# Keeping all five W_q blocks of the first group in SBUF, with a smaller weight store, in a two-layer decode kernel

## Chip, cores and metric

The kernel runs on one core of one Trainium2 chip. The metric is device time in microseconds (us): the median of the runs of the whole program, lower is better. The program before takes 736.22 us (median of 3 runs, 736.16 to 736.47).

## What is computed

Four rows of 640 floats pass twice through the same two sublayers, all in float32 and with the same weights in both layers: a layer norm, attention over the last 1024 positions of a key and value cache (32 heads of 128), and a projection; then a layer norm and a gated MLP with 1728 hidden units. Each sublayer adds to its input.

```python
def _A_ref(x, k_cache, v_cache, wq, wo):        # B=4, D=640, Hq=32, Dh=128, W=1024
    q = (x @ wq) ...                            # per head
    scores = einsum("bhqd,bhkd->bhqk", q, k[last W]) * Dh ** -0.5
    o = einsum("bhqk,bhkd->bhqd", softmax(scores), v[last W])
    return o @ wo
def _B_ref(x, W_gate, W_up, W_down):
    gate = x @ W_gate; gate = gate * (gate > 0)
    return (gate * (x @ W_up)) @ W_down
x = x + _A_ref(_layernorm(x), ...); x = x + _B_ref(_layernorm(x), ...)   # twice
```

## The kernel before

**Data.** Host code lays all weights and caches out as three rows of 128 partitions: `heads` (groups 0 to 6 of heads, 255,744 floats a partition), `kept` (the last two groups, 47,360 floats) and `mlp` (25,920 floats). "Floats" below always counts floats per partition; one float on 128 partitions is 512 bytes. The nine groups hold 4, 4, 4, 4, 4, 4, 3, 3 and 2 heads (`HEADS`, L27). Line 38 sets the order inside `heads`: W_q and keys of the first group, then for each group g the W_q of g+2, the keys of g+1, the output weights of g-1 and the values of g. A head has 4096 floats of keys, 4096 of values and 640 of output weights; W_q of a group of four has 2560, in five blocks of 512.

**Store.** SBUF holds one large tile, `store` (53,888 floats, L103), and `first_q` (1024 floats, L104), which keeps the first two of the five W_q blocks of group 0 from the start to the end, so that layer 1 reads them again without a load. Everything else passes through `store`. `load()` (L157) walks a fixed list of pieces (L130 to L147) and issues one DMA for each on SP's queue, in that order and on no other queue. `heads` and `mlp` pieces go to the running position `at`, which starts at `FIRST` and goes back to 0 at the end of the store; a large piece is cut at the marks in `QUARTERS`. `kept` pieces always go to their own place, 0 to 47,360 (`FRONT`), and stay for layer 1, where groups 7 and 8 come first. The first `kept` piece is W_q of groups 7 and 8, 3200 floats to places 3200 to 6400, and it stands in the list just before the keys of group 6 (L131; `turn[0]` is the start of these keys). During the first MLP, whose pieces go through the ring between `FRONT` and the end of the store, the `kept` part is resident.

**What a load waits for.** The Python list `live` notes which places hold data that no instruction has read yet. `done()` frees places after a block's matmul has been emitted, and calls `load()` again, which issues the next piece only if the whole target is free (only at a few places, with `part=True`, may it take a shorter piece). So a piece is issued behind the last reader of what lies in its place, and all later pieces stand behind it. Here "block" is 512 floats with the one matmul that reads them, which TensorE runs as two passes, so that a count in the profile is twice the number of blocks.

**Order on TensorE.** For each group g of a layer (L422): transposes of the softmax rows, W_q of g+2 (`query`, L317 and L322), keys of g+1 (`scores`, L346), output weights of g-1 (`project`, L404), values of g (`values`, L374). The MLP (L446) goes through the blocks of its four column groups (L458), then of W_down (L493, L502). Small per-row numbers (sums, maxima, reciprocals) live in tiles of one or 16 floats.

Of the kernel before, what the change touches and what calls it, by code (L numbers as in the profile page):

```python
# [7 lines left out]
F32 = mybir.dt.float32  # L8
# [4 lines left out]
B, D, H, DH, W, F = 4, 640, 32, 128, 1024, 1728  # L13
P = 128
KC = D // P
# [12 lines left out]
SIDE = 4  # L28
# [28 lines left out]

HELD = 1024  # L60
STORE = 53888
QUARTERS = [STORE // 4, STORE // 2, STORE // 4 * 3, STORE]
FRONT = KEPT * 2 * (D + KV)
FIRST, FIRST_MLP = 10944, 53248


def size_of(what, i):
# [23 lines left out]
def decode_kernel(ctx: ExitStack, tc: tile.TileContext, x, source, sel, out):  # L91
    nc = tc.nc
    const = ctx.enter_context(tc.tile_pool(name="const", bufs=1))
    work = ctx.enter_context(tc.tile_pool(name="work", bufs=1))
    small = ctx.enter_context(tc.tile_pool(name="small", bufs=2))
    ps_s = ctx.enter_context(tc.tile_pool(name="ps_s", bufs=1, space=bass.MemoryType.PSUM))
    ps_p = ctx.enter_context(tc.tile_pool(name="ps_p", bufs=2, space=bass.MemoryType.PSUM))
    ps_o = ctx.enter_context(tc.tile_pool(name="ps_o", bufs=1, space=bass.MemoryType.PSUM))
    ps_y = ctx.enter_context(tc.tile_pool(name="ps_y", bufs=1, space=bass.MemoryType.PSUM))
    ps_m = ctx.enter_context(tc.tile_pool(name="ps_m", bufs=2, space=bass.MemoryType.PSUM))  # L100
    big = ctx.enter_context(tc.tile_pool(name="big", bufs=1))
    big.tile([P, 8], F32, name="pad")
# [34 lines left out]
    pieces(0, "kept", 0, 2 * D, 4 * D, KEPT * D)  # L137
    pieces(0, "mlp", 0, 1152, *range(GU0, WD0 + 1, 1280), WD1, *range(WD1 + 2 * D, MLP - D, 2 * D), MLP - D, MLP)
    k = at_part("k", 0)
    pieces(1, "heads", HELD, 2560, 3584, k, *range(k + 1536, k + 4 * 1536 + 1, 1536))  # L140
    wanted = [3072, 6144, 9216, 13312, 17408, 22016, 27136, 32256, 38912]
    pieces(1, "heads", k + 4 * 1536, *[max(c for c in ROWS["heads"][2] if c <= k + 4 * 1536 + w) for w in wanted],
           k + 50176)
# [13 lines left out]
    def load(part=False):  # L157

        nonlocal at, spare
        if not held:  # L160
            nc.sync.dma_start(out=first_q, in_=source["heads"][:, :HELD])
        while todo:
# [66 lines left out]
    xT = const.tile([P, KC * B + 28], F32, name="xT")  # L229


    qT = const.tile([P, SIDE - 1 + SIDE * SIDE * B], F32, name="qT")
    GAP = SIDE * B - B
    pT = [const.tile([P, GAP + 8 * SIDE * B], F32, name=f"pT{i}") for i in range(2)]
    for t in xT, qT, *pT:
# [6 lines left out]
    eps_sb = const.tile([P, 1], F32, name="eps_sb")  # L242
    nc.vector.memset(eps_sb, EPS)

    ident, sel_q = sel_sb[:, :P], sel_sb[:, P:]
# [25 lines left out]
    def normalized():  # L271

        ysb, xc, sq = probs[:, :QUARTER], gates[:, :QUARTER], gates[:, QUARTER:2 * QUARTER]
        waits[0] = True
        su = small.tile([P, 1], F32, name="su", bufs=1)
# [5 lines left out]
        ss = small.tile([P, 1], F32, name="ss", bufs=1)  # L281
# [8 lines left out]
        nc.vector.tensor_copy(xT[:, :KC * B].rearrange("p (c b) -> p c b", b=B), pt[:, :, :B])  # L290
        return ss

    def deviation(ss):
        var = mean(ss, "var")
        rs = small.tile([P, 1], F32, name="rstd")
        nc.scalar.activation(rs, var, AF.Sqrt, bias=eps_sb)
        nc.vector.reciprocal(rs, rs)
        return rs

    def table(func):  # L300

        t = small.tile([P, 1], F32, name="t", bufs=1)
        nc.scalar.activation(t, eps_sb, func)

    def go_on():

# [2 lines left out]
    qp, nm, sums, pps, r, oT = {}, {}, {}, {}, {}, {}  # L309
# [29 lines left out]
    def scores(layer, g):  # L339
        n = len(HEADS[g])  # L340
        for i, h in enumerate(HEADS[g]):
            for j in range(2):
                for b in range(B):
                    lo = (j * B + b) * 512
                    at = SIDE - 1 + SIDE * (B * i + b) - i
                    nc.tensor.matmul(ps[32 * b:32 * b + SIDE, j, :], qT[:, at:at + SIDE], part(layer, "k", h, lo, 512),  # L346
                                     start=i == 0, stop=i == n - 1, tile_position=(0, 32 * b))
                    part_done(layer, "k", h, lo, 512)
        nm[g] = small.tile([P, 1], F32, name="nm")
        nc.vector.tensor_reduce(nm[g], ps.rearrange("p j n -> p (j n)"), axis=AX.X, op=ALU.max, negate=True)  # L350

    def softmax(g):
        sums[g] = small.tile([P, 1], F32, name="sm")
# [54 lines left out]
    def attention(layer):  # L408
        gs = order[layer]
        load(True)  # L410
        rstd = deviation(normalized())
        table(AF.Exp)
        query(layer, gs[0], True)
        query_out(gs[0], rstd)
        query(layer, gs[1])
        query_turned(gs[0])
        go_on()
        query_out(gs[1], rstd)
        scores(layer, gs[0])
        softmax(gs[0])  # L420
        query_turned(gs[1])
        for before, g, after, then in zip([None] + gs, gs, gs[1:] + [None], gs[2:] + [None] * 2):  # L422
            totals(g)
            turned(g)
            if before is not None:
                values_turned(before)
            if then is not None:
                query(layer, then)
                query_out(then, rstd)
            if after is not None:  # L430
                scores(layer, after)
                softmax(after)
            else:
                table(AF.Sqrt)
            if then is not None:
                query_turned(then)

            if before is not None and not (layer == 0 and after is None):
                project(layer, before)
            values(layer, g, after is None)  # L440
        values_turned(gs[-1])
        if layer == 0:
            project(layer, gs[-2])
        project(layer, gs[-1], True)

    def forward(layer):  # L446
        load(True)
        ss = normalized()
        gus, hTs = {}, {}

        def gate(j):
# [21 lines left out]
            return b  # L473

        def hidden(j, h):
            hTs[j] = small.tile([P, 4, B], F32, name="hT", bufs=4)
            ph = ps_m.tile([P, 4, 32], F32, tag="m", name="ph")
            if j < 3:
                nc.tensor.transpose(ph, h, ident)
                nc.vector.tensor_copy(hTs[j], ph[:, :, :B])  # L480
                return

            for g, lo, f in (0, 0, 0), (1, 64, 0), (2, 0, 1), (2, 64, 1):
                nc.tensor.matmul(ph[lo:lo + 64, f, :B], h, ident[:96, 32 * g:32 * g + B],
                                 start=True, stop=True, tile_position=(0, lo))
            nc.vector.tensor_copy(hTs[j][:, :2], ph[:, :2, :B])
# [18 lines left out]

        gate(3)
        waits[0] = layer == 0
        rstd = deviation(ss)
        go_on()
        h = gated(3)  # L510
        for j, j1 in (3, 0), (0, 1), (1, 2):
# [72 lines left out]
```

## Time and profile before

| what | number |
|---|---|
| median of 3 runs | 736.22 us |
| the profiled execution, its own time | 736.33 us |
| its span (first to last instruction) | 734.5 us |
| TensorE matmul, busy | 452.5 us (62%) |
| VectorE, ScalarE busy | 75.0 us, 47.1 us |
| mean granted TensorE clock | 0.83 |
| read from HBM | 312.24 MB, 425 GB/s over the span |

The profile is of one execution on the chip. Busy time is given by engine; PEld is TensorE's weight load, SPq is SP's queue, from which the DMAs are issued. The line "DMA" gives the share of time in which the 16 DMA engines were busy. A row of the timeline has the start, the length, the engine, the line, what is written and read, the count, and in brackets the engine's idle time before and what ended it. A row of DMA issues has the target and source, the count, the size of one and the time from issue to landing.

### The profile page before, as it was taken

The numbers are of one execution on the slowest core, as the hardware profiler recorded it, in microseconds if no ns is written. First come the engines' busy times: TensorE is split into PE (matmuls) and PEld (weight loads), VectorE is DVE, ScalarE is ACT, GpSimd is POOL, SyncE is SP. The second block draws the span as 40 slices with busy tenths as digits, with TensorE's granted clock in tenths as the row PEclk, the third lists the DMA queues.
The fourth block names the chain that finished last, engine by engine and source line by source line (L and its number), as shares of the span: only waits on it lengthen the run. The fifth ranks groups of instructions, "written<-read, shape, count | busy, mean of one in ns | idle before, by whom it ended". The sixth has DMA issues, their size and how long they took to land.

```text
span 734.5 us, 8243 instructions
## 1 busy us (share of the span) xinstructions
PE 452.5 (62%) x3749; PEld 142.7 (19%) x3749; DVE 75.0 (10%) x279; ACT 47.1 (6%) x88; POOL 0.2 (0%) x4
## 2 busy tenths in 40 slices
PE   1657366555566635727789897446756545656686
PEld 0111111111121201202233231101211111122242
DVE  1011010010000101101101221001010100001010
ACT  1100000000000000000101110000000000000110
POOL 0000000000000000000000000000000000000000
PEclk9989787867678887969899999867878977668897
DMA  9999999999999999999999999999999999999996
GB/s 380 454 421 430 452 430 422 429 446 434 417 444 445 408 446 419 438 433 419 419 405 406 432 433 431 445 432 443 431 427 425 447 432 424 435 445 429 420 427 285
DMA packets 15738, 312.85 MB, mean 426 GB/s; under 512 B 1748, under 2 KB 2132, under 8 KB 7512
## 3 DMA queue, kind: packets, MB, share of 16 engines
q1 hardware_dynamic: 15552, 312.24, 99.1%
q8 instruction: 29, 0.48, 0.2%
q10 hardware_dynamic: 152, 0.09, 0.1%
q14 instruction: 5, 0.04, 0.0%
HBM read 312.24 MB, written 0.08 MB: 425 GB/s over the span
## 4 chain that ended last, share of the span: by engine, by line
DMA 54%; PE 30%; another core or an unknown queue 14%; issue 1%; DVE 1%; ACT 0%; SPq 0%; DVEq 0%; ACTq 0%
DMA store<-in_heads 32%; PE ps L346 12%; DMA store<-in_mlp 12%; DMA store<-in_kept 10%; PE po L374 9%; PE y L404 1%; PE qp L317 1%; PE pp L359 1%; PE qp L322 1%; PE gu L458 1%; PE qt L334 1%; PE ot L394 0%; PE po L259 0%; PE y L493 0%
## 5 line engine op out<-in xcount | busy, mean ns | idle before, releaser
L346 PE MATMUL ps<-store,qT 128*4 128x512 f32 x1024 | 160.9, 700 | 108.2 <-DMA store<-in_heads 104.3
L374 PE MATMUL po<-store,pT 128*16 128x512 f32 x1024 | 155.2, 718 | 105.4 <-DMA store<-in_heads 95.4
L374 PEld LDWEIGHTS po<-store,pT 128*16 128x16 f32 x1024 | 35.0, 110 | 210.8 <-issue 128.3
L346 PEld LDWEIGHTS ps<-store,qT 128*4 128x4 f32 x1024 | 29.4, 94 | 221.6 <-DMA store<-in_heads 119.9
L350 DVE TENSOR_REDUCE nm<-ps 128x1 f32<-128x1024 f32 x18 | 22.0, 1224 | 245.0 <-PE ps L346 245.0
L354 ACT ACTIVATE probs<-ps,nm 128x1024 f32<-128x1024 f32 x18 | 20.1, 1114 | 353.6 <-DVE nm L350 345.9
L317 PE MATMUL qp<-store,xT 128*32 128x512 f32 (+2 forms) x136 | 22.9, 614 | 24.7 <-DMA store<-in_heads 24.6
L404 PE MATMUL y<-store,oT 128*4 128x160 f32 x512 | 26.2, 335 | 8.7 <-DMA store<-in_heads 7.6
L458 PE MATMUL gu<-store,xT 128*32 128x256 f32 (+1 forms) x300 | 26.3, 414 | 8.3 <-DMA store<-in_mlp 7.9
L370 DVE COPY pT<-pp 128x16 f32<-128x16 f32 x128 | 17.1, 168 | 135.3 <-PE po L374 135.3
L381 ACT COPY gates<-po 128x512 f32<-128x512 f32 x16 | 9.4, 587 | 243.1 <-PE po L374 243.1
L359 PE MATMUL pp<-sel_sb,probs 128*128 128x128 f32 x144 | 19.5, 281 | 0.0
L322 PE MATMUL qp<-store,xT 128*32 128x512 f32 (+4 forms) x48 | 17.7, 514 | 0.0
L327 DVE TENSOR_SCALAR gates<-qp,rstd 128x512 f32<-128x512 f32 (+2 forms) x18 | 12.4, 691 | 48.4 <-PE qp L322 44.4
L359 PEld LDWEIGHTS pp<-sel_sb,probs 128*128 128x128 f32 x144 | 17.1, 146 | 0.0
L404 PEld LDWEIGHTS y<-store,oT 128*4 128x4 f32 x512 | 13.3, 93 | 19.5 <-DMA store<-in_heads 8.0
L387 DVE RECIPROCAL r<-so 128x16 f32<-128x16 f32 x18 | 4.6, 257 | 121.4 <-PE so L385 121.4
L458 PEld LDWEIGHTS gu<-store,xT 128*32 128x32 f32 x300 | 11.4, 123 | 18.9 <-issue 8.7
L394 PE MATMUL ot<-sel_sb,gates 128*128 128x128 f32 x72 | 11.7, 283 | 1.2 <-DVE gates L378 1.2
L334 PE MATMUL qt<-sel_sb,gates 128*128 128x128 f32 x64 | 12.3, 316 | 0.0
L493 PE MATMUL y<-store,hT 128*4 128x160 f32 x208 | 10.6, 305 | 1.7 <-DMA store<-in_mlp 1.7
L334 PEld LDWEIGHTS qt<-sel_sb,gates 128*128 128x128 f32 x64 | 7.6, 155 | 18.8 <-issue 17.5
(62 smaller groups left out, 107.2 us busy)
## 6 DMA issues: line engine op xcount, KB each, us to landing
store<-in_heads SPq DMA_DIRECT2D x18, 6656.0 KB, 54.0
store<-in_heads SPq DMA_DIRECT2D x7, 6912.0 KB, 52.0
store<-in_heads SPq DMA_DIRECT2D x2, 6592.0 KB, 54.4
store<-in_heads SPq DMA_DIRECT2D x2, 5376.0 KB, 65.4
store<-in_mlp SPq DMA_DIRECT2D x16, 640.0 KB, 6.9
store<-in_kept SPq DMA_DIRECT2D x4, 2048.0 KB, 39.9
store<-in_heads SPq DMA_DIRECT2D x3, 2560.0 KB, 22.0
store<-in_heads SPq DMA_DIRECT2D x1, 6896.0 KB, 46.1
```

The lines of the kernel that those rows point to most:

```text
L317: nc.tensor.matmul(qp[g][32 * c:32 * c + 32, :], xT[:, B * c:B * c + 32], part(layer, "q", g, c * n, n), start=True, stop=c > 0 and not sp ...
L322: nc.tensor.matmul(qp[g][32 * a:32 * a + 32, a * m:a * m + m], xT[:, B * c:B * c + 32], part(layer, "q", g, c * n + a * m, m), start=False ...
L327: nc.vector.tensor_scalar(gates[:, :len(HEADS[g]) * P], qp.pop(g), rstd, SCALE, op0=ALU.mult, op1=ALU.mult)
L334: nc.tensor.transpose(qt[:, i], gates[:, i * P:(i + 1) * P], ident)
L346: nc.tensor.matmul(ps[32 * b:32 * b + SIDE, j, :], qT[:, at:at + SIDE], part(layer, "k", h, lo, 512), start=i == 0, stop=i == n - 1, tile_ ...
L350: nc.vector.tensor_reduce(nm[g], ps.rearrange("p j n -> p (j n)"), axis=AX.X, op=ALU.max, negate=True)
L354: nc.scalar.activation(probs, ps.rearrange("p j n -> p (j n)"), AF.Exp, bias=nm.pop(g), accum_out=sums[g])
L359: nc.tensor.transpose(pps[g][c // 4][:, c % 4, :], probs[:, c * P:(c + 1) * P], ident)
L370: nc.vector.tensor_copy(to[:, 4 * j:4 * j + 4], pp[j][:, :, i:P:32])
L374: nc.tensor.matmul(po[32 * a:32 * a + SIDE * B, :], t[:, at:at + SIDE * B], part(layer, "v", h, c * 512, 512), start=i == 0 and c < 4, sto ...
L404: nc.tensor.matmul(y[32 * a:32 * a + B], o[:, i], part(layer, "o", h, a * QUARTER, QUARTER), start=False, stop=last and h == HEADS[g][-1], ...
L458: nc.tensor.matmul(gus[j][32 * g:32 * g + 32, :2 * n], xT[:, B * c:B * c + 32], get(layer, "mlp", lo, 2 * n), start=c == 0, stop=c == KC - ...
```

## The change

`first_q` grows from 1024 to 2560 floats (all five blocks), and the store shrinks from 53,888 to 52,480. The marks in `QUARTERS` move, `FIRST` goes from 10,944 to 10,752 and the start of the first MLP to the last 640 floats of the smaller store, so that the ring of the first MLP between 47,360 and the end of the store has 5120 floats where it had 6528. Layer 1 loads `heads` from float 2560 on, not from 1024. To make room, the one-float tiles become columns of the tile `qT`, and `r`, `oT` and `hT` share four buffers.

```diff
-HELD = 1024
-STORE = 53888
-QUARTERS = [STORE // 4, STORE // 2, STORE // 4 * 3, STORE]
+HELD = KC * 4 * P
+STORE = 55040 - HELD
+QUARTERS = [13312, 2 * 13312, 3 * 13312, STORE]
-FIRST, FIRST_MLP = 10944, 53248
+FIRST, FIRST_MLP = 10752, STORE - 640
...
-    small = ctx.enter_context(tc.tile_pool(name="small", bufs=2))
+    small = ctx.enter_context(tc.tile_pool(name="small", bufs=4))
...
-    pieces(1, "heads", HELD, 2560, 3584, k, *range(k + 1536, k + 4 * 1536 + 1, 1536))
+    pieces(1, "heads", HELD, 3584, k, *range(k + 1536, k + 4 * 1536 + 1, 1536))
...
-    qT = const.tile([P, SIDE - 1 + SIDE * SIDE * B], F32, name="qT")
+    n = SIDE - 1 + SIDE * SIDE * B
+    qT = const.tile([P, n + 10], F32, name="qT")
+    ones = qT[:, n:]
+    qT = qT[:, :n]
...
+    eps_sb, su, ss, t1 = (ones[:, i:i + 1] for i in range(4))
+    rstds, nms, sms = ([ones[:, i + j:i + j + 1] for j in range(2)] for i in (4, 6, 8))
...
-        nm[g] = small.tile([P, 1], F32, name="nm")
+        nm[g] = nms[g % 2]
...
-        r[g] = small.tile([P, SIDE, B], F32, name="r")
+        r[g] = small.tile([P, 4, B], F32, tag="s", name="r")
...
-        oT[g] = small.tile([P, SIDE, B], F32, name="oT")
+        oT[g] = small.tile([P, 4, B], F32, tag="s", name="oT")
...
-            hTs[j] = small.tile([P, 4, B], F32, name="hT", bufs=4)
+            hTs[j] = small.tile([P, 4, B], F32, tag="s", name="hT")
```

The new sizes move where each piece lands in the store. The rows below give an instruction's line, kind, target and source, shape, and the semaphores it waits for: `DMAHW0` to `DMAHW7` tell that a DMA has landed (they are used in turn), `PE` that TensorE has passed a point. First SP's queue where the first `kept` piece stands, before:

```order
L186 DMA store<-in_heads 128x13824 [waits DMAHW7_49,DMAHW6_49,PE_49]
L186 DMA store<-in_heads 128x13312 [waits PE_49]
L186 DMA store<-in_heads 128x3072 [waits DMAHW0_49,PE_49]
L186 DMA store<-in_kept 128x3200 [waits PE_49]
L186 DMA store<-in_heads 128x6656 [waits PE_49]
L186 DMA store<-in_heads 128x13824 [waits DMAHW2_49,DMAHW1_49,PE_49]
L186 DMA store<-in_heads 128x10752 [waits PE_49]
```

And the same place of the changed kernel:

```order
L186 DMA store<-in_heads 128x13312 [waits DMAHW6_49,PE_49]
L186 DMA store<-in_heads 128x12288 [waits DMAHW7_49,PE_49]
L186 DMA store<-in_heads 128x7168 [waits DMAHW0_49,PE_49]
L186 DMA store<-in_kept 128x3200 [waits DMAHW4_49,PE_49]
L186 DMA store<-in_heads 128x6656 [waits PE_49]
L186 DMA store<-in_heads 128x13312 [waits DMAHW1_49]
L186 DMA store<-in_heads 128x11264 [waits DMAHW2_49]
```

The `heads` piece ahead of the `kept` one goes to the start of the store and has 7168 floats now, 3072 before; the `kept` row has gained a wait for a landing, `DMAHW4`.

On TensorE, the reader of that last `heads` piece is `values` of group 4 (L374). Before, its second half:

```order
L374 MATMUL po<-store,pT_99 16x512 x3
L374 MATMUL po<-store,pT_100 16x512 [waits DVE_49]
L374 MATMUL po<-store,pT_100 16x512
L374 MATMUL po<-store,pT_100 16x512 [waits DMAHW4_49]
L374 MATMUL po<-store,pT_100 16x512
L374 MATMUL po<-store,pT_100 16x512 [waits DVE_49]
L374 MATMUL po<-store,pT_100 16x512 x3
```

and in the changed kernel, with the group's third and fourth head whole:

```order
L374 MATMUL po<-store,pT_99 16x512 [waits DVE_49]
L374 MATMUL po<-store,pT_99 16x512
L374 MATMUL po<-store,pT_99 16x512 [waits DMAHW4_49]
L374 MATMUL po<-store,pT_99 16x512
L374 MATMUL po<-store,pT_99 16x512 [waits DVE_49]
L374 MATMUL po<-store,pT_99 16x512 x3
L374 MATMUL po<-store,pT_100 16x512 [waits DVE_49]
L374 MATMUL po<-store,pT_100 16x512 x3
L374 MATMUL po<-store,pT_100 16x512 [waits DVE_49]
L374 MATMUL po<-store,pT_100 16x512 x3
```

The wait for `DMAHW4` stands ahead of the last 14 blocks of the group now, ahead of the last six before.

Last, SP's queue at the start of the first MLP, as one piece of the difference:

```order
 L186 DMA store<-in_mlp 128x1280 [waits DMAHW3_49]
 L186 DMA store<-in_mlp 128x1280 [waits DMAHW4_49]
-L186 DMA store<-in_mlp 128x1280 [waits DMAHW5_49]
-L186 DMA store<-in_mlp 128x768 [waits DMAHW6_49]
-L186 DMA store<-in_mlp 128x512 [waits DMAHW7_49,DMAHW0_49,PE_49]
-L186 DMA store<-in_mlp 128x768 [waits DMAHW2_49,DMAHW1_49,PE_49]
+L186 DMA store<-in_mlp 128x512 [waits DMAHW5_49]
+L186 DMA store<-in_mlp 128x768 [waits DMAHW6_49,DMAHW0_49,PE_49]
+L186 DMA store<-in_mlp 128x768 [waits DMAHW2_49,DMAHW7_49,DMAHW1_49,PE_49]
 L186 DMA store<-in_mlp 128x512 [waits PE_49]
```

The first piece that waits for TensorE (`PE`) stands behind 4992 floats of this MLP now and behind 6528 before.

More of the change, by code (lines that the diff above doesn't have):

```diff
@@ L101, in decode_kernel @@
     big = ctx.enter_context(tc.tile_pool(name="big", bufs=1))
-    big.tile([P, 8], F32, name="pad")
+    big.tile([P, 16], F32, name="pad")
     store = big.tile([P, STORE], F32, name="store")
@@ L241, in decode_kernel @@
     nc.vector.memset(po, 0.0)
-    eps_sb = const.tile([P, 1], F32, name="eps_sb")
+    eps_sb, su, ss, t1 = (ones[:, i:i + 1] for i in range(4))
+    rstds, nms, sms = ([ones[:, i + j:i + j + 1] for j in range(2)] for i in (4, 6, 8))
     nc.vector.memset(eps_sb, EPS)
@@ L274, in normalized @@
         waits[0] = True
-        su = small.tile([P, 1], F32, name="su", bufs=1)
         nc.vector.tensor_reduce(su, y, axis=AX.X, op=ALU.add)
@@ L280, in normalized @@
         nc.vector.tensor_tensor(xc, ysb, mu.to_broadcast([P, QUARTER]), op=ALU.subtract)
-        ss = small.tile([P, 1], F32, name="ss", bufs=1)
         nc.scalar.activation(sq, xc, AF.Square, accum_out=ss)
@@ L290, in normalized, with deviation @@
         nc.vector.tensor_copy(xT[:, :KC * B].rearrange("p (c b) -> p c b", b=B), pt[:, :, :B])
-        return ss
-    def deviation(ss):
+    def deviation():
         var = mean(ss, "var")
-        rs = small.tile([P, 1], F32, name="rstd")
+        rs = rstds[0]
+        rstds.reverse()
         nc.scalar.activation(rs, var, AF.Sqrt, bias=eps_sb)
@@ L300, in table @@
     def table(func):
-        t = small.tile([P, 1], F32, name="t", bufs=1)
-        nc.scalar.activation(t, eps_sb, func)
+        nc.scalar.activation(t1, eps_sb, func)
     def go_on():
@@ L348, in scores @@
                     part_done(layer, "k", h, lo, 512)
-        nm[g] = small.tile([P, 1], F32, name="nm")
+        nm[g] = nms[g % 2]
         nc.vector.tensor_reduce(nm[g], ps.rearrange("p j n -> p (j n)"), axis=AX.X, op=ALU.max, negate=True)
     def softmax(g):
-        sums[g] = small.tile([P, 1], F32, name="sm")
+        sums[g] = sms[g % 2]
         nc.scalar.activation(probs, ps.rearrange("p j n -> p (j n)"), AF.Exp, bias=nm.pop(g), accum_out=sums[g])
@@ L410, in attention @@
         load(True)
-        rstd = deviation(normalized())
+        normalized()
+        rstd = deviation()
         table(AF.Exp)
@@ L447, in forward @@
         load(True)
-        ss = normalized()
+        normalized()
         gus, hTs = {}, {}
@@ L507, in forward @@
         waits[0] = layer == 0
-        rstd = deviation(ss)
+        rstd = deviation()
         go_on()
```

## The prediction, as it was made

> **What bounds the kernel now.** I read the page's first two parts first, to see which resource never rests.
>
> ```profile
> PE 452.5 (62%) x3749; PEld 142.7 (19%) x3749; DVE 75.0 (10%) x279; ACT 47.1 (6%) x88; POOL 0.2 (0%) x4
> DMA  9999999999999999999999999999999999999996
> ```
>
> TensorE is busy 62% of the span and VectorE 10%, but the DMA engines are full in every slice except the last. The windows say how full, from 20 us to the end of the loads, and in the stretch of layer 0 that the sum below needs:
>
> ```profile
> 20.00:725.00 705.00, 442.40 (x3596) 138.46 (x3588) 70.94 (x263) 42.57 (x82) 0.00 (x0) 0.82 1.00 430
> 100.00:340.00 240.00, 139.60 (x1070) 40.42 (x1074) 21.33 (x82) 10.75 (x18) 0.00 (x0) 0.78 1.00 431
> ```
>
> The last two columns are the DMA share and GB/s: 1.00 and 430 over 705 us. So the kernel is one unbroken stream of loads, and what follows the last of them is short. The chain of waits shows that end:
>
> ```profile
> 708.31 22.62 DMA store<-in_mlp
> 730.98 0.50 PE y L493 x8
> 731.50 0.32 DVE probs L524
> ```
>
> The last load lands at 730.9; matmuls and a copy of under 1 us follow, then the store of the output. Two things can therefore move the time: the number of bytes, and any moment in which the queue has nothing to transfer. A wait of TensorE by itself costs nothing.
>
> **What is removed.** Layer 1 no longer loads floats 1024 to 2560 of `heads`: 1536 floats x 512 bytes = 0.786 MB. At 430 GB/s that is **1.8 us** off the stream. Layer 0 loads the same bytes as before. At the start only the cut changes (2560 floats for `first_q`, not 1024), and TensorE is far from needing them:
>
> ```profile
> first_q<-in_heads SPq DMA_DIRECT2D x1, 512.0 KB, 3.9
> 18.17 1.07 PE L317 MATMUL qp<-first_q,xT 128*32 128x512 f32 x2 [0.20 <-DVE xT L290]
> ```
>
> The 1536 further floats land 1.8 us after 0.7 + 3.9 = 4.6 us, and the first reader starts at 18.2.
>
> **What is added: an empty queue ahead of the first `kept` piece.** The order rows of SP give the places. In the changed kernel `heads` fills the store from 10,752 to 52,224 in the first lap, to 52,224 in the second and third, and to 52,096 in the fourth; of the 207,744 floats ahead of the keys of group 6, 7168 are left, and they go to places 0 to 7168. They are the last 14 blocks of the values of group 4. The next piece in the list is `kept`, with places 3200 to 6400. These are inside the 7168. So this load can't be issued before the piece just ahead of it has landed and all but one of its 14 blocks have been read; hence the new `DMAHW4` in its row. SP's queue is in order, and all later loads stand behind it: the keys of group 6, two pieces of 13,312 and 11,264 floats, and so on. When the 7168 floats have landed, nothing is in flight. Before, the piece had 3072 floats, below 3200, and the target held only floats read long ago. The issue times show what is lost:
>
> ```profile
> 204.01 0.33 SPq L186 DMA_DIRECT2D store<-in_heads  x1
> 205.71 0.33 SPq L186 DMA_DIRECT2D store<-in_kept  x1
> ```
>
> ```profile
> store<-in_heads SPq DMA_DIRECT2D x1, 1536.0 KB, 46.3
> ```
>
> ```profile
> store<-in_kept SPq DMA_DIRECT2D x1, 1600.0 KB, 48.4
> ```
>
> The `heads` piece of 3072 floats (1536 KB) is issued at 204.0 and lands 46.3 us later, at 250.3; the `kept` piece is issued at 205.7, with 44.6 us of transfers ahead of it, and lands at 254.1. In the changed kernel the bytes up to this point are the same, so the 7168 floats land at 250.3 too, and only then does the reading begin.
>
> How fast TensorE reads them depends on its clock, so I look at this very place before:
>
> ```profile
> 231.06 6.94 PE L346 MATMUL ps<-store,qT 128*4 128x512 f32 x44 [6.84 <-DMA store<-in_heads]
> 237.93 0.55 PE L334 MATMUL qt<-sel_sb,gates 128*128 128x128 f32 x3
> 238.41 1.27 PE L404 MATMUL y<-store,oT 128*4 128x160 f32 x32
> 246.83 9.32 PE L374 MATMUL po<-store,pT 128*16 128x512 f32 x64 [7.15 <-DMA store<-in_heads]
> 257.64 0.85 PE L317 MATMUL qp<-store,xT 128*32 128x384 f32 x8
> ```
>
> ```profile
> 246.80:251.80 5.00, 4.97 (x28) 1.26 (x32) 0.35 (x2) 0.00 (x0) 0.00 (x0) 0.54 1.02 433
> 251.80:256.10 4.30, 4.30 (x45) 0.97 (x33) 0.35 (x2) 0.00 (x0) 0.00 (x0) 1.00 1.05 452
> ```
>
> After 7 us of idling TensorE gets half the clock for 5 us (0.54), then the full one. The weight loads show the pace in both states:
>
> ```profile
> 250.20 0.19 PEld L374 LDWEIGHTS po<-store,pT 128*16 128x16 f32 x4 [0.66 <-issue]
> 251.05 0.19 PEld L374 LDWEIGHTS po<-store,pT 128*16 128x16 f32 x4 [0.66 <-DVE pT L370]
> 252.53 0.12 PEld L374 LDWEIGHTS po<-store,pT 128*16 128x16 f32 x4 [0.31 <-issue]
> 252.96 0.12 PEld L374 LDWEIGHTS po<-store,pT 128*16 128x16 f32 x4 [0.31 <-DVE pT L370]
> ```
>
> Four passes are two blocks: 0.85 us at half clock, 0.43 at full, so 0.43 and 0.215 us a block. In the changed kernel the piece of 12,288 floats ahead lands 7168 x 512 bytes / 431 GB/s = 8.5 us earlier, at 241.8, and TensorE restarts there, at half clock until about 246.8. It has the last block of keys, the transposes and the projection to do (some 2 us at full clock by the rows above, 4 at half), then 18 blocks of values, two of them by 246.8 and 16 at 0.215: it is through at about 250.2, as the last piece lands, and goes on at full clock. The 13th block of it starts 12 x 0.215 = 2.6 us later and takes
>
> ```profile
> L374 PE MATMUL po<-store,pT x64: 592/592/1061, 246.8 to 255.6; 128*16 128x512 f32 x64
> ```
>
> 0.6 us at full clock and 1.06 at half (ns, least, median and most), so SP is released at 250.3 + 3.2 = **253.5**.
>
> What a load pays on an empty queue is not shown in mid-kernel. The nearest rows are the first load and the last store:
>
> ```profile
> 0.73 0.38 SPq L161 DMA_DIRECT2D first_q<-in_heads  x1
> 1.20:1.70 0.50, 0.00 (x0) 0.00 (x0) 0.29 (x2) 0.00 (x0) 0.00 (x0) 1.00 0.13 10
> 1.70:2.20 0.50, 0.00 (x0) 0.00 (x0) 0.50 (x1) 0.00 (x0) 0.00 (x0) 1.00 1.19 141
> ```
>
> ```profile
> out_x<-probs SPq DMA_DIRECT2D x1, 80.0 KB, 1.6
> ```
>
> `first_q` (0.52 MB) takes 3.9 us, 1.2 of them transfer at 430 GB/s: 2.7 us of latency, with no bytes for the first 1.0 us. The output (0.08 MB, 0.2 us) leaves 1.4 us. I take 2.4, nearer to the load, since a load it is; the ends 1.4 and 2.7 stay for the range. The Trainium skill ("DMA: Bandwidth & Descriptors", Specifications) gives about 0.6 us to the first byte for DMAs issued from SP; by it the restart would cost some 0.4 us less than by the start shown here, and the sum would be 739.6.
>
> The `kept` piece (3200 floats, 1.64 MB, 3.8 us at 431 GB/s) then lands at 253.5 + 2.4 + 3.8 = 259.7, not at 254.1: **5.6 us** later, and all that follows with it, since the stream has no other hole from which to take them back. (Ends: 4.6 and 5.9.) That TensorE waits for these floats at 257.6 adds nothing of its own.
>
> **The smaller ring of the first MLP.** This is the other place where the queue is short.
>
> ```profile
> store<-in_mlp SPq DMA_DIRECT2D x5, 640.0 KB, 5.9
> ```
>
> ```profile
> store<-in_mlp SPq DMA_DIRECT2D x16, 640.0 KB, 6.9
> ```
>
> ```profile
> 380.00:391.00 11.00, 10.81 (x116) 4.03 (x115) 0.86 (x4) 0.73 (x2) 0.00 (x0) 1.00 1.00 399
> ```
>
> The first row is of the issues from 380 to 391 us, the second of all pieces of this size, the third of the traffic in those 11 us. There a piece of 1280 floats lands 5.9 us after its issue; 1.6 of that are its own bytes at 399 GB/s and 1.4 to 2.7 latency, so 1.6 to 2.9 us are queueing behind others. The ring loses 1408 floats, 1.8 us at that rate. What is left is between -0.2 and 1.1 us. I take no hole, and keep up to 2 us over the stretch for a rival.
>
> **The small tiles.** The order shows as many waits on VectorE and ScalarE as before, of the same kinds, and no new instruction; both engines idle for most of the span. Cost 0; the cover is their idle time, and a wait of 0.3 us a group on them would still be behind the stream.
>
> **Sum.** The profiled execution took 736.33 us of its own, 1.8 beyond its span. 736.33 - 1.8 + 5.6 = 740.1; that execution is 0.1 above the median, so the forecast is **740.0 us**, slower by 0.5%.
>
> **The rivals.**
>
> *Half clock at the release.* If TensorE falls back to half clock while it waits for the last piece, 13 blocks take 12 x 0.43 + 1.06 = 6.2 us and not 3.2. For it: the clock was at 0.54 just after the idle time before 246.8. Against it: here the idle time comes 8 us earlier. Time: 740.0 + 3.0 + 0.3 (the dear restart) = 743.3. Chance 0.14.
>
> *The ring starves as well.* If a piece of the first MLP needs more lead than I gave it, a few holes of some tenths add 1 to 2 us: 741.5. For it: the margin's lower end is below zero. Against it: over the whole MLP the median is 6.9 us, a microsecond more room than in these 11 us. Chance 0.14.
>
> *The stream makes up for it (the other side).* If the transfers after the hole ran faster than the 430 GB/s before, the hole would be paid back: 476 us follow it, so 435 GB/s in place of 430, 1.2%, returns 5.5 us, and at that point the kernel ends at 734.5, faster by the saved bytes. It decides from 433.5 GB/s, which gives back the 3.8 us that the forecast adds. For it: 452 GB/s stands in a row above. Against it: that is a window of 4 us, and the rate is 431 over 240 us with 45 us of loads queued, so an empty moment is no reason for a higher one. The Trainium skill (the same page and section) puts the fabric's ceiling at 435 GB/s and an HBM limit of about 358 per core; the 430 here is over the second, so only the first can hold, and by it at most these 5.5 us could come back. Chance 0.05.
>
> *A quick restart.* If TensorE has cleared the blocks at 253.1 and the restart costs only 0.5 us, the delay is 3.3 us and the time 737.7, at the edge of no change; it needs a latency below a third of the smallest row. Chance 0.05.
>
> **How the numbers follow.** Forecast 740.0, chance 0.62; its own ends are 739.0 (restart 1.4) and 740.3 (2.7), a little wider for the clock. The range 738.2 to 743.4 takes in the forecast and the first two rivals, 0.9 together, and leaves out the quick restart and the made-up hole. A run of this kernel tells 0.2% (1.5 us) from no change. Faster 0.05, same 0.05, slower 0.90.
>
> **What would show it.** In the profile after: a slice of the DMA line near 250 us below 9; the `kept` piece of 1600 KB landing about 6 us after its issue, not 48; its issue near 253.5, released by TensorE at L374; TensorE waiting for `kept` ahead of the W_q of group 7; 311.45 MB read. The ring is judged by the GB/s from 370 to 410 and the landing time of the 640 KB pieces (about 4.1 in the tight stretch). The forecast is wrong if the queue is full at 250 us, if the hole is far from 5.6 us, or if there is a second one.

## The result, and the profile after

The changed kernel takes **747.45 us** (median of 6 runs, 746.44 to 750.96) and the kernel before 736.31 (736.16 to 736.69): a ratio of 1.0161, 95% interval 1.0137 to 1.0185. It is slower by 11.1 us, where 3.7 were forecast, and the time lies beyond the range. The profiled execution took 747.22 us, 10.9 more than that of before, at the same distance of 1.8 us from its span. (Two of the six runs took 750.29 and 750.96 us; no trace shows what they add.)

The page after: the DMA line, the rate in the 40 slices, and the bytes.

```profile
DMA  9999999999999699999999999999999999999996
GB/s 391 438 421 455 420 435 445 414 443 436 423 440 422 268 453 412 434 424 433 417 382 348 394 433 431 448 434 429 435 435 429 429 446 420 433 438 433 420 429 274
HBM read 311.45 MB, written 0.08 MB: 418 GB/s over the span
```

The same rate line of before:

```profile
GB/s 380 454 421 430 452 430 422 429 446 434 417 444 445 408 446 419 438 433 419 419 405 406 432 433 431 445 432 443 431 427 425 447 432 424 435 445 429 420 427 285
```

There are two dips, not one. The 14th slice (268) is the forecast hole. Slices 21 to 23 (382, 348, 394) are the first MLP and the start of layer 1, and the DMA line, which has a 6 for the hole, shows nothing of them: its digit stays at 9. The share of busy time hides a stream that limps; the GB/s show it.

How much each dip costs follows from two windows. After, in the columns that the prediction explained (last two: DMA share, GB/s):

```profile
249.00:256.00 7.00, 6.45 (x61) 2.55 (x53) 1.01 (x5) 0.59 (x1) 0.00 (x0) 1.00 0.17 33
360.00:440.00 80.00, 65.77 (x698) 25.17 (x698) 12.51 (x45) 10.30 (x23) 0.00 (x0) 1.00 0.99 389
```

and before:

```profile
249.00:256.00 7.00, 7.00 (x56) 1.64 (x48) 0.52 (x3) 0.00 (x0) 0.00 (x0) 0.83 1.05 446
360.00:440.00 80.00, 71.08 (x760) 27.04 (x758) 13.55 (x46) 10.03 (x23) 0.00 (x0) 1.00 1.02 419
```

At 431 GB/s the hole has lost (446 - 33) x 7 / 431 = 6.7 us, and the 80 us around the first MLP another (419 - 389) x 80 / 431 = **5.6 us**. With the 1.8 us saved that makes 10.5 of the 10.9. I use the second formula for several runs below, and call its result the loss around the MLP. It is of the one execution that was profiled, which can be some us from the median of its runs.

The chain of waits says what the second dip is made of. Its rows (some of them) have the start, the length and what ran. After, from the last load before the MLP on:

```profile
349.18 21.32 DMA store<-in_kept
373.67 3.91 DMA store<-in_mlp
377.62 0.67 PE gu L459 x6
378.30 6.15 DMA store<-in_mlp
384.50 1.06 PE gu L459 x10
385.58 6.41 DMA store<-in_mlp
392.04 0.63 PE gu L459 x4
393.03 0.58 PE gu L459 x5
393.63 5.22 DMA store<-in_mlp
398.89 0.47 PE y L494 x6
399.37 5.62 DMA store<-in_mlp
411.78 5.38 PE ps L346 x48
```

Load, reading, load in the same place or the one behind it, and so on: each DMA is on the path from its issue to its landing, and the next one starts when TensorE has read the first. Call such a step a lap. From 378.30 to 399.37 there are three laps of 7.0 us on average. 5120 floats are 2.62 MB, which is 6.1 us at 431 GB/s. A lap that takes longer than the ring's contents last cannot keep the stream full. The second and third lap hand on less than the whole ring, since the pieces don't fit its end evenly: the issues on the chain are of floats 9600, 14,720, 19,520 and 23,360 of the row, 13,760 in three laps. At 431 GB/s these take 16.3 us, and here 21.1. Before, the same chain:

```profile
361.85 9.36 DMA store<-in_mlp
371.25 1.06 PE gu L458 x10
372.33 6.93 DMA store<-in_mlp
383.39 1.17 PE gu L458 x8
384.94 1.11 PE gu L458 x8
388.90 5.68 DMA store<-in_mlp
```

Here too some loads are on the path, but with matmuls of L458 between them that run on data already landed, and 6528 floats last 7.8 us, longer than such a lap.

### The profile page after: what moved, and what is told of

It is laid out like the page before. It is cut to its first block, busy times and chain, and to the rows that moved or that the text cites. A ratio compares the mean times of both kernels' runs of the same rounds, so it can differ in the third digit from the quotient of the medians.

```text
span 745.4 us, 8245 instructions
## 1 busy us (share of the span) xinstructions
PE 467.2 (63%) x3749; PEld 143.8 (19%) x3749; DVE 75.1 (10%) x279; ACT 47.1 (6%) x88; POOL 0.2 (0%) x4
## 3 DMA queue, kind: packets, MB, share of 16 engines
q1 hardware_dynamic: 15408, 311.45, 98.0%
HBM read 311.45 MB, written 0.08 MB: 418 GB/s over the span
## 4 chain that ended last, share of the span: by engine, by line
DMA 48%; PE 34%; another core or an unknown queue 15%; issue 1%; DVE 1%; SPq 0%; ACT 0%; DVEq 0%; ACTq 0%
DMA store<-in_heads 33%; PE ps L346 14%; PE po L374 11%; DMA store<-in_kept 9%; DMA store<-in_mlp 7%; PE y L404 2%; PE qp L317 1%; PE qt L334 1%; PE pp L359 1%; PE qp L322 1%; PE ot L394 1%; PE gu L459 0%; SPq L186 0%; PE y L494 0%
## 5 line engine op out<-in xcount | busy, mean ns | idle before, releaser
L346 PE MATMUL ps<-store,qT 128*4 128x512 f32 x1024 | 175.5, 743 | 119.0 <-DMA store<-in_heads 114.6
L374 PE MATMUL po<-store,pT 128*16 128x512 f32 x1024 | 151.9, 706 | 75.9 <-DMA store<-in_heads 66.8
L374 PEld LDWEIGHTS po<-store,pT 128*16 128x16 f32 x1024 | 34.9, 110 | 179.2 <-issue 97.2
L350 DVE TENSOR_REDUCE qT<-ps 128x1 f32<-128x1024 f32 x18 | 22.0, 1225 | 269.7 <-PE ps L346 269.7
L354 ACT ACTIVATE probs<-ps,qT 128x1024 f32<-128x1024 f32 x18 | 20.1, 1114 | 391.9 <-DVE qT L350 384.2
L404 PE MATMUL y<-store,oT 128*4 128x160 f32 x512 | 25.8, 332 | 16.3 <-DMA store<-in_heads 15.2
L322 PE MATMUL qp<-store,xT 128*32 128x512 f32 (+3 forms) x38 | 17.9, 585 | 4.0 <-DMA store<-in_heads 4.0
L327 DVE TENSOR_SCALAR gates<-qp,qT 128x512 f32<-128x512 f32 (+2 forms) x18 | 12.4, 690 | 65.4 <-PE qp L322 61.5
L359 PEld LDWEIGHTS pp<-sel_sb,probs 128*128 128x128 f32 x144 | 16.3, 140 | 0.0
```

The source lines that it names most:

```text
L322: nc.tensor.matmul(qp[g][32 * a:32 * a + 32, a * m:a * m + m], xT[:, B * c:B * c + 32], part(layer, "q", g, c * n + a * m, m), start=False ...
L359: nc.tensor.transpose(pps[g][c // 4][:, c % 4, :], probs[:, c * P:(c + 1) * P], ident)
L374: nc.tensor.matmul(po[32 * a:32 * a + SIDE * B, :], t[:, at:at + SIDE * B], part(layer, "v", h, c * 512, 512), start=i == 0 and c < 4, sto ...
L404: nc.tensor.matmul(y[32 * a:32 * a + B], o[:, i], part(layer, "o", h, a * QUARTER, QUARTER), start=False, stop=last and h == HEADS[g][-1], ...
```

## Experiments

Each ratio is against runs of the kernel before that were taken beside that run; their medians lie between 736.10 and 736.90 us. Where two runs had different ones, their distances from their own are compared.

**The first four runs** ask whether there are two losses (theory A: the hole and the ring, each by itself) or one that brings the other. *Only the hole:* the kernel before with one number changed, which puts the last `heads` piece onto the places of the first `kept` piece.

```diff
-FIRST, FIRST_MLP = 10944, 53248
+FIRST, FIRST_MLP = 15040, 53248
```

> The kernel before with FIRST = 15040, so that the heads piece ahead of the first kept piece has 7168 floats, as in the changed kernel; the ring of the first MLP, first_q and the small tiles stay. Theory A (three separate terms: the hole costs 6.2 us, the smaller ring 6.3 us, the bytes give back 1.8): 736.3 + 6.2 = 742.5, between 741.5 and 743.5, and full DMA from 370 to 420 us. Theory B (the hole leaves the DMA engines or TensorE out of step, and the ring starves only for that reason): 746 to 748, with GB/s below 380 in the first MLP here as well.

Measured 742.55 us, ratio 1.0070 (1.0054 to 1.0087). Its windows:

```profile
249.00:256.00 7.00, 6.26 (x53) 2.84 (x45) 0.94 (x5) 0.59 (x1) 0.00 (x0) 1.00 0.20 49
360.00:440.00 80.00, 67.76 (x705) 24.66 (x704) 12.26 (x44) 9.27 (x22) 0.00 (x0) 0.98 1.02 419
```

(446 - 49) x 7 / 431 = 6.4 us in the hole, and 419 GB/s around the MLP, the same as before. The hole costs what the time shows, 5.7 us against the 736.90 of the kernel before beside it, and does not starve the ring.

*No hole:* the changed kernel with the first lap moved, so that no `heads` piece ahead of the first `kept` piece lies on its places.

```diff
-FIRST, FIRST_MLP = 10752, STORE - 640
+FIRST, FIRST_MLP = 7168, STORE - 640
```

> The changed kernel with FIRST = 7168, so that the piece ahead of the first kept piece has 3072 floats and does not reach place 3200; all else as changed. Theory A: 747.4 - 6.2 = 741.2, between 740 and 742.5, with the same low GB/s in the first MLP. Theory B: the ring does not starve without the hole, so 734.5 to 736.

Measured 742.75 us, ratio 1.0076 (1.0048 to 1.0104).

```profile
249.00:256.00 7.00, 7.00 (x65) 2.58 (x58) 0.78 (x4) 0.59 (x1) 0.00 (x0) 0.99 1.03 439
360.00:440.00 80.00, 67.15 (x681) 25.36 (x677) 11.53 (x38) 8.24 (x20) 0.00 (x0) 0.91 0.96 370
```

The hole is gone (439 GB/s) and the loss around the MLP is still there, 9.1 us, 7.3 after the saved bytes (the profiled execution took 743.79). So the second loss is not a consequence of the first. In this trace it is larger than with the hole (5.6), and the mean clock is 0.91, against 1.00. The times do not show such a difference: *only the hole* and *no hole* lose 5.7 and 5.9 us by their medians, 11.5 together, and the changed kernel, which has both, loses 11.1.

*Only the ring:* the kernel before, with the first MLP and the first pieces of layer 1 kept below a mark at 5120 floats.

```diff
-FIRST, FIRST_MLP = 10944, 53248
+FIRST, FIRST_MLP = 10944, 51840
+TOP = FRONT + 5120
...
-            ends = QUARTERS if end - lo > 16384 else [STORE]
-            room = min(e - to for e in ends if e - to >= 2048 or e == STORE)
+            top = TOP if (row == "mlp" and layer == 0) or (layer == 1 and spare) else STORE
+            ends = QUARTERS if end - lo > 16384 else [top]
+            room = min(e - to for e in ends if e - to >= 2048 or e == top)
```

> The kernel before, but the pieces of the first MLP and the first lap of layer 1 may only use the 5120 floats behind the kept part (of 6528); no hole, first_q and small tiles as before. Theory A: 736.3 + 6.3 = 742.6, between 741 and 744. Theory B: no more than 738.

Measured 744.33 us, ratio 1.0098 (1.0074 to 1.0122): 7.4 us, a little beyond theory A's upper end.

```profile
360.00:440.00 80.00, 66.02 (x649) 24.18 (x644) 11.53 (x38) 8.23 (x20) 0.00 (x0) 0.89 0.95 364
```

A loss of 10.2 us around the MLP, and the profiled execution (746.51, the slowest of its four) was 10.2 above that of before. Against *no hole*, which has the same ring and saves the bytes, the medians differ by 1.6 us. That is near the forecast's 1.8, but the two sets of runs overlap (741.33 to 745.20, 743.26 to 746.51), so these times alone do not show it.

*Only the small tiles:* all sizes of before, the tiles of the changed kernel. Two of its lines:

```diff
-    qT = const.tile([P, SIDE - 1 + SIDE * SIDE * B], F32, name="qT")
+    qT = const.tile([P, n + 10], F32, name="qT")
...
-        oT[g] = small.tile([P, SIDE, B], F32, name="oT")
+        oT[g] = small.tile([P, 4, B], F32, tag="s", name="oT")
```

> The changed kernel with the sizes of before (first_q 1024, store 53888, FIRST and the first MLP's place as before): only the one-float tiles in qT and the shared buffers are left of the change. Theories A and B: 736.3, within 0.5. Theory C (sharing buffers or columns of qT adds waits that delay the release of the ring's places): 738 to 742, with longer waits on VectorE or ScalarE in the first MLP.

Measured 736.37 us, ratio 0.9994 (0.9984 to 1.0005). They cost nothing.

**The ring's length.** Theory D: the ring is lead time, and the loss falls steeply to nothing near 6500 floats. Theory E: it does not. First 5760 floats (the edit of *only the ring* with `TOP = FRONT + 5760` and `FIRST_MLP` 52,480):

> As ring_only, but with 5760 floats for the first MLP and the first lap of layer 1 (6528 before, 5120 in ring_only). Theory D (a place is used again only after its reading, 1.0 us to the first byte, the slowest of 16 DMA engines and its landing: a cycle of some 6.5 to 7.5 us, so the loss grows steadily below the 6528 floats that 7.8 us of transfer fill): between 738 and 741. Theory E (a ring that merely holds too few whole 1280-float pieces, four in place of five): 5760 holds four as well, so 743 to 744.5, as ring_only.

Measured 742.48 us, ratio 1.0076 (1.0061 to 1.0091): by the time, theory D seems to fall. The landing times, compared with those of before at the same float of the same row (the end of the piece that ends there), say more. They are worked out from the issue and semaphore records of the traces (us later than before):

```
                    kept    heads   mlp     mlp     heads  heads   last
                    W_q g7  end L0  17,280  end     11,264 28,672  load
after               +6.2    +6.4    +8.2    +10.4   +9.8   +10.6   +10.9
hole_only           +5.8    +6.4    +6.2    +6.3    +6.8   +6.7    +6.4
no_hole             -0.3    +0.3    +3.5    +7.1    +7.9   +7.7    +7.5
ring_only           -0.4    +0.2    +3.3    +6.4    +8.9   +9.8    +10.2
ring_5760           -0.3    +0.2    +0.9    +1.4    +4.2   +4.3    +4.0
ring_5760_aligned   -0.3    +0.2    +0.2    +1.6    +2.4   +2.8    +3.0
nohole_fine         -0.3    +0.1    +1.5    +2.1    -0.1   +1.6    +1.2
held512             -0.4     0.0    +0.1    -0.2    +1.4   +1.6    +1.8
held1536            -0.6    -0.1    +0.2    +0.2    +3.4   +3.4    +3.1
held1536_aligned    -0.4    +0.1    +0.1    +0.1    -1.4   +1.1    +1.7
```

The rows stand for the profiled executions, not for the medians. Inside the MLP, 5760 floats lose 1.2 us where 5120 lose 4.0 to 6.8: steep, as D has it. Another 2.8 us are lost at the jump to layer 1. (This execution, 740.20 us, was the fastest of four; the others took 742.23 to 742.73, and where they lose 2 us more no trace shows.) With this length the last MLP pieces wrap and end in mid-ring, so layer 1's first `heads` pieces, which start at 47,360, lie on pieces that have just landed. I had mixed the length with the place of the wrap. In the next two runs that change the length the last pieces end in mid-ring as well: one block kept (`HELD = 512`, a ring of 7040, 0.6 us more to load),

> The kernel before with first_q of 512 floats and a store of 54,400, so that the ring has 7040: layer 1 loads 512 floats (0.262 MB, 0.6 us) more. Theory D: if 6528 floats already lose a little, the larger ring gives some of it back: 736.1 to 736.9. Below 735.8 the ring before loses over 1 us.

738.47 us, ratio 1.0030 (1.0020 to 1.0041), and three blocks kept (`HELD = 1536`, 6144) with smaller pieces and without the fillers that the *fillers* runs below describe:

> The changed kernel with first_q of 1536 floats, a store of 53,504 (ring 6144), FIRST = 7168 so that no hole comes, the finer pieces, and without the keep-busy transposes of the first MLP: 512 floats less to load than before (0.6 us). Theory D: the ring's loss at 6144 with finer pieces is below 1 us, so 735.5 to 736.7; a version to beat the kernel before if the loss is under 0.6.

739.57 us, ratio 1.0045 (1.0033 to 1.0057). Both missed, yet inside the MLP they lose -0.2 and 0.3 us; the rest comes at the jump. In the second the fillers are missing too, so the wrap need not be all of it. Two more runs move the start of the MLP, so that its last piece ends at or near the ring's end; the first moves nothing else. For 5760 floats:

```diff
-FIRST, FIRST_MLP = 10944, 52480
+FIRST, FIRST_MLP = 10944, 49920
```

> The kernel before with a ring of 5760 floats in the first MLP, as in the earlier run with that ring, but the MLP's first piece at float 49,920 of the store, so that its last piece ends where the ring ends, and layer 1's first pieces fall on the places read longest ago. Theory D (the ring is lead time: 5760 floats last 6.9 us, and a cycle of reading, issue, latency and the spread of the 16 DMA engines takes 6.5 to 7.5): the first MLP loses about 1.4 us as in the earlier run and the jump to layer 1 nothing, 737.8 us (737.2 to 738.6). Theory E (what was lost at the jump belongs to the shorter ring itself, wherever its pieces end): 742 to 743 again.

Measured 739.28 us, ratio 1.0045 (1.0033 to 1.0058), apart from the 1.0076 of the other start: by the medians this one number is worth 3.2 us. (The two profiled executions, 740.20 and 739.28, are only 0.9 apart, so the traces show less of it than the times.) It is 0.7 above theory D's end, since the jump still loses 0.8. Around the MLP, with the start at 52,480:

```profile
360.00:440.00 80.00, 69.86 (x746) 25.86 (x741) 13.23 (x44) 9.57 (x23) 0.00 (x0) 1.00 0.98 394
```

and at 49,920:

```profile
360.00:440.00 80.00, 69.22 (x744) 25.46 (x739) 13.20 (x44) 9.44 (x22) 0.00 (x0) 1.00 1.01 405
```

For three blocks, with the fillers put back as well:

```diff
-FIRST, FIRST_MLP = 7168, STORE - 640
+FIRST, FIRST_MLP = 7168, 51584
...
-        waits[0] = False
+        waits[0] = layer == 0
```

> The changed kernel with three W_q blocks kept (1536 floats), so that the ring has 6144 floats; pieces of 640 to 1024 floats in the first MLP and at the start of layer 1; no heads piece ahead of the first kept piece falls on its places; and the MLP begins at float 51,584, so that its last piece ends near the end of the store. Theory D: 6144 floats last 7.3 us, the smaller pieces shorten the cycle, so the MLP loses 0.2 us or less and the jump nothing, and the 0.26 MB less to read give back 0.6: 735.9 us (735.3 to 736.6), the same as before or faster by a hair. Theory E (a ring below 6528 floats starves layer 1's first lap whatever the places): 739 to 740, as in the earlier run with this ring.

Measured 736.73 us, ratio 1.0005 (0.9996 to 1.0014): the same as before, as D has it, though not faster, and the median is 0.1 above its range. Two things were changed at once here, the start and the fillers, and the fillers alone are worth some 3 us in a kernel with pieces of this size (below). So this run does not show what the start is worth; the pair at 5760 floats does. From *held1536*:

```profile
360.00:440.00 80.00, 68.07 (x714) 23.11 (x712) 13.37 (x44) 9.43 (x22) 0.00 (x0) 0.94 0.98 397
```

to this one the loss around the MLP falls from 4.1 to 1.9 us:

```profile
360.00:440.00 80.00, 70.66 (x731) 25.18 (x729) 13.21 (x44) 9.43 (x22) 0.00 (x0) 0.96 1.02 409
```

Nothing is late by the jump (-1.4); 2.5 us come later in layer 1's first lap, and the saved 0.6 does not pay for them in this execution. (It took 738.00 us; five of the eleven runs took 736.03 to 736.21.) No version here beats the kernel before.

**The lap.** If a lap is reading, issue and landing, pieces of about half the size shorten it at the same ring. *No hole* with pieces of 768, 640 and 1024 floats:

```diff
-    pieces(0, "mlp", 0, 1152, *range(GU0, WD0 + 1, 1280), WD1, *range(WD1 + 2 * D, MLP - D, 2 * D), MLP - D, MLP)
+    pieces(0, "mlp", 0, 1152, *range(GU0, WD0 + 1, 768), WD1, *range(WD1 + D, MLP + 1, D))
-    pieces(1, "heads", HELD, 3584, k, *range(k + 1536, k + 4 * 1536 + 1, 1536))
+    pieces(1, "heads", HELD, 3584, 4608, k, *range(k + 1024, k + 4 * 1536 + 1, 1024))
```

> no_hole with finer pieces: 768 floats for the gate and up weights (1280 before), 640 for the down weights, and 1024 at the start of layer 1 (1536). Theory D: reading, transfer and release of one piece get some 1.0 to 1.3 us shorter, so most of the ring's loss goes: 736 to 739. Rival F (each DMA has a cost of its own and only eight can be under way, so more and smaller ones make it worse): 743 or more.

Measured 738.83 us, ratio 1.0030 (1.0018 to 1.0042): the distance from the kernel before falls from 5.9 to 2.5 us.

```profile
360.00:440.00 80.00, 69.18 (x743) 24.87 (x737) 13.22 (x44) 9.44 (x22) 0.00 (x0) 1.00 1.01 404
```

370 has become 404 GB/s with the same 5120 floats (the profiled executions, 743.79 and 737.54, are further apart than the medians). So the ring is not too small for the bytes; it is too small for the lap. What became shorter is hardly the landing: the pieces of 384 and 320 KB take

```profile
store<-in_mlp SPq DMA_DIRECT2D x19, 384.0 KB, 5.7
store<-in_mlp SPq DMA_DIRECT2D x15, 320.0 KB, 5.4
```

where those of 640 KB in *no hole* take 5.7 from 376 to 400 us. It is the time in which TensorE reads. On the chain of waits three laps of *no hole* (issues at 369.81 and 395.73) take 8.6 us on average, of which 2.7 lie between a landing and the next issue; with the fine pieces (372.10 and 392.95) it is 7.0 us, with 1.3 between. Part of that can be the clock, 0.91 against 1.00 in the two windows. The same pieces in the kernel before, where the ring is long enough, should gain nothing:

> The kernel before with the same finer pieces. Theory D: the ring of 6528 is about at its limit, so 735.5 to 737. Rival F: 738 or more.

Measured 736.92 us, ratio 1.0010 (1.0000 to 1.0019). They gain nothing.

*Fillers.* `busy()` (L259 after) puts idle transposes on TensorE in the first MLP, which keep its clock up and lie in the lap. They leave with one line:

```diff
-        waits[0] = layer == 0
+        waits[0] = False
```

In *no hole*:

> no_hole without the transposes that only keep TensorE busy in the first MLP (waits[0] = False there; the result of these transposes is used nowhere). Theory D: a piece is read 0.4 to 0.7 us sooner and its place released that much earlier, so 739 to 741.5. If the release does not matter, or TensorE's clock falls without them: 742.7 or more.

740.95 us, ratio 1.0070 (1.0054 to 1.0087): nearer to the kernel before by 1.3 us, but the two intervals overlap, so no gain is shown. The clock from 360 to 440 us is 0.91 with the fillers and without. In *no hole* with the fine pieces:

> nohole_fine without the transposes that only keep TensorE busy in the first MLP. Theory D: the two ways to shorten the cycle add up in part, 737 to 738. If the release is no longer what the ring waits for: 738.8.

741.64 us, ratio 1.0065 (1.0051 to 1.0078): a miss, 3.1 us further from the kernel before than with fillers.

```profile
360.00:440.00 80.00, 66.64 (x666) 22.48 (x664) 12.25 (x39) 8.23 (x20) 0.00 (x0) 0.89 0.99 384
```

The clock is 0.89 here and 1.00 with them. In the kernel before:

> The kernel before without the same transposes. Theory D: at 6528 floats the release decides little, 735.5 to 736.6. If TensorE's lower clock without them counts at the start of layer 1: 737 or more.

736.73 us, ratio 1.0013 (1.0003 to 1.0023), between the two theories. I had counted the fillers as a cost of the lap alone. With the fine pieces they also held the clock; that reading is faster for it is the likely reason for the 3.1 us, but no run changes the clock and nothing else.

## Why the prediction was wrong, step by step

- **The stream as the bound:** right. 432 GB/s from 424 to 736 us after; what was lost, was lost ahead of that.

```profile
424.00:736.00 312.00, 203.19 (x1607) 63.10 (x1603) 31.20 (x121) 18.41 (x35) 0.00 (x0) 0.81 1.00 432
```

  Before, the same stretch, 8 to 11 us earlier:

```profile
416.00:725.00 309.00, 197.11 (x1585) 63.63 (x1583) 31.18 (x121) 18.44 (x35) 0.00 (x0) 0.81 1.00 432
```

  The rate is the same, so the rival in which the stream makes up for the hole did not come.
- **Saved bytes, -1.8:** the bytes are right (311.45 against 312.24 MB). For the time there is only the 1.6 us between two medians with the same ring, whose runs overlap.
- **The hole, +5.6:** right in mechanism and nearly in size; the hole alone cost 5.7 us in its own run. The rows of SP's queue, of the clock, and of the DMA issues after:

```profile
202.19 0.33 SPq L186 DMA_DIRECT2D store<-in_heads  x1
253.94 0.33 SPq L186 DMA_DIRECT2D store<-in_kept  x1
```

```profile
250.00:254.00 4.00, 4.00 (x42) 1.04 (x33) 0.17 (x1) 0.00 (x0) 0.00 (x0) 1.00 0.00 0
```

```profile
store<-in_kept SPq DMA_DIRECT2D x1, 1600.0 KB, 6.4
```

  The `kept` piece is issued at 253.94, not 253.5, at full clock (1.00, so the rival of the half clock did not come), and lands 6.4 us later: 3.8 of transfer and 2.6 of latency, where I took 2.4. It lands at 260.3, 6.2 us later than before, so this term is 0.6 short.
- **The small tiles, 0:** right.
- **The ring, "I take no hole":** this is the step that failed, and it makes up most of the miss of 7.1 us (747.22 against 740.1); the hole's 0.6 is next. The ring costs 5.6 us here by the windows and 6.3 by the landing times. The forecast read the landing time of 5.9 us as own bytes, latency, and "1.6 to 2.9 us" of queueing, which a shorter ring could give back. It gave back 0.3: the pieces in the tight stretch after land in

```profile
store<-in_mlp SPq DMA_DIRECT2D x10, 640.0 KB, 5.6
```

  5.6 us, not in the 4.1 that I named, though the stream is starving. Nor did half-size pieces land much sooner (5.4 and 5.7). So the 5.9 could not be treated as slack; what holds it up is open (see the last section). And the step left out the other half of the lap: a place is free only when its piece has been read. With 5.6 for the landing, one lap is some 7 us by the chain, and 5120 floats last 6.1. Such a shortfall is not paid once but in each lap. SP's waits from 366 to 412 us show where the stream stood, after:

```profile
SPq L186 <- DMA store<-in_mlp: 10.2, 11, 2.8
```

  and before:

```profile
SPq L186 <- DMA store<-in_mlp: 5.0, 6, 1.6
```

  The total, the number and the longest of the waits for MLP pieces to land have all grown, the first two to about double.
- **The rival "the ring starves as well":** the right mechanism with a chance of 0.14 and a price of 1 to 2 us. I worked its price out of the same false slack, and put down "a microsecond more room" over the whole MLP as evidence against it. The 6.9 us there take in the start of the MLP, where SP runs ahead of TensorE and a piece lands up to 9.4 us after its issue (361.85 in the chain above); near the end it is 5.7 (388.90). The longer times are loads waiting in the queue, not room for a shorter ring.

By the table, 4.0 us go in the MLP (+6.4 to +10.4), and 2.3, once the saved 1.8 are added back, behind it (+10.4 to +10.9), for the most part in layer 1's first lap through the same places.

## What to carry to other kernels

A buffer ring has to last as long as one whole lap: wait for the reader, issue, and landing under load. Take the landing time in the tight stretch as it stands, and do not subtract "queueing" from it unless a row shows a piece of that size landing faster in the same traffic. Look at GB/s by stretch, not at the DMA share. And when a ring changes its length, look at where its last piece ends, because what comes next may have to wait for it.

## What the runs showed of the hardware

- **A landing is the slowest of 16.** Each load raises its semaphore 16 times, and the records show when. Some rows of the first MLP (us; in the semaphore records, not in a view of the profile):

```
                  issue    floats  first of 16   last of 16   spread
before            360.32   1280    366.78        369.66       2.88
before            387.05   1280    391.30        392.99       1.69
no_hole           360.59   1280    366.80        369.96       3.16
no_hole           379.09   1280    382.94        385.72       2.77
no_hole           388.48   1280    391.89        392.43       0.54
after             380.38   1280    384.68        385.97       1.29
hole_only         253.72   3200    259.44        259.95       0.51
```

  In these rows the 16 increments are up to 3.2 us apart in the stream, and 0.5 us right behind an empty queue (hole_only) and in one row of the starving stretch of *no hole*. In the changed kernel, for issues from 380 to 402 us, the first increment comes 3.4 to 4.6 us after the issue and the last one 1.3 to 2.2 later. So of a landing time of 5.6 us the greater part has passed before the first engine is done. No run changed either part by itself, so what sets them stays open.
- **Latency on an empty queue in mid-kernel is 2.4 to 2.6 us** for a load from SP: the landing of the `kept` piece, 6.4 us in the changed kernel and 6.2 in *only the hole* (253.72 to 259.95), less the 3.8 that its bytes take at 431 GB/s, which makes it an estimate. The Trainium skill ("SBUF — State Buffer", The DMA setup-cost knee) gives about 2 us plus the bytes at 436 GB/s, 5.8 us for this piece as an estimate; the 6.4 measured is 0.6 longer.
- **Behind a wait of 5 us the clock was at half.** After the hole TensorE waits for `kept`,

```profile
260.45 1.51 PE L317 MATMUL qp<-store,xT 128*32 128x384 f32 x8 [5.01 <-DMA store<-in_kept]
```

  and runs at half the clock for the next 5 us:

```profile
261.00:266.00 5.00, 2.19 (x10) 0.35 (x2) 0.62 (x1) 0.00 (x0) 0.00 (x0) 0.50 0.99 426
```

  In *only the hole*, after a wait of 4.83 us for the same piece, the mean clock is 0.81 over these 5 us and 0.53 over the next 5, so two runs answer such a wait differently. Here a full stream follows and nothing is lost by it. That a half clock lengthens the lap of a short ring is argued; the changed kernel starves with the clock at 1.00 from 360 to 440 us, so it is not needed for that.
